# Attention over a 32,768-key cache on one core: the values of heads 8, 12 and 16 loaded by GpSimd's queue instead of SP's

## The chip, the cores and the metric

The kernel runs on one core of one Trainium2 chip. Time is device microseconds from the start to the end of the program. TensorE is called PE, VectorE DVE, ScalarE ACT, GpSimd POOL and SyncE SP. SP computes nothing here; it issues DMA transfers, which 16 DMA engines carry out.

## The reference

One decoding step for one token: a layer norm, attention with 32 heads over a cache, and a small dense block behind it. Only the first part matters here.

```python
def _A_ref(x, k_cache, v_cache, wq, wo):
    B, Sq, D = x.shape                     # 1, 1, 512
    H, Dh = 32, 128                        # k_cache, v_cache: (1, 32, 32768, 128)
    q = (x @ wq).reshape(B, Sq, H, Dh).transpose(0, 2, 1, 3)
    scores = jnp.einsum("bhqd,bhkd->bhqk", q, k_cache) * (Dh ** -0.5)
    p = _softmax(scores, axis=-1)
    o = jnp.einsum("bhqk,bhkd->bhqd", p, v_cache)
    return o.transpose(0, 2, 1, 3).reshape(B, Sq, H * Dh) @ wo

h = x + _A_ref(_layernorm(x), k_cache, v_cache, wq, wo)
return h + _B_ref(_layernorm(h), w1, b1, w2)   # 512 -> 1376 -> 512
```

All tensors are bf16. Each head reads 8.39 MB of keys and as much of values, each once: 537 MB over 32 heads.

## The kernel before

**Tiles.** SBUF holds a ring of six slots of 128 partitions x 16,384 values. The keys of one head fill two slots, and there are two such homes for keys, taken by even and odd heads. The values of one head fill two more slots, and there is one home for values (`V_HOME`). Partition p holds the rows 256 p to 256 p + 255 of the head, so a partition's share is one run of 64 KB in memory and in SBUF.

**Work of one head h.** `head(h)`: PE transposes the 256 key blocks (`k_group`, into tile `tps`), DVE copies each eight of them to SBUF (tile `ering`), and PE multiplies these by the query into the scores (`scores`, tile `sps`). DVE then takes the maximum. `rest`: while the exponentials of head h-1 are ready, PE runs the product with the values of head h-1 (`pv`, 256 matmuls into tile `ops`, "PV" below), with the small matmuls of the softmax of head h in between; then ACT makes the exponentials of head h (tile `pbuf`). So PE's order is: keys of head h, PV of head h-1, keys of head h+1, PV of head h, and so on.

**The order of the loads.** The list `order` in the builder gives it: the query weights (`WQ`), the keys of head 0, and then, for each h from 1, the keys of h and the values of h-1. In `program`, SP goes through this list. Before each load it waits until the buffer is free: keys of head h+2 wait for the transposes of head h (`freed_by`), values of head h wait for the end of PV of head h-1 (the event `pv{h-1}`, through `done_with`). `start` then issues the load, which raises the semaphore `ready[slot]` by 16 when it has landed. SP issues in list order: while it waits for one buffer, nothing behind it in the list is issued. PE waits on `ready[V_HOME]` before the first matmul of PV, against a count that `fills` gives for each load.

Some loads at the beginning and the end are cut in pieces (`pieces`); those of heads 8, 12 and 16 are whole.

**POOL** has two small steps at the start of the program (`iota`, `memset`) and one multiplication near its end (`hu`).

## Time and profile before

| | |
|---|---|
| time, median of 2 runs | 1275.15 us (1275.08 to 1275.23) |
| profiled execution, span from the first to the last instruction | 1273.1 us |
| mean granted PE clock | 0.766 |
| read from memory | 548.09 MB, 431 GB/s over the span |
| busy: PE, DVE, ACT, POOL | 1019.9, 718.2, 20.6, 0.9 us |

The profile gives for its execution the span alone; the median of the runs is 2.05 us above it. How to read the rows: an engine's name with a "q" (SPq) is its instruction queue, here the issuing of DMAs; "tile <- tile" names what an instruction writes and reads; L551 is the line of the kernel at which it was issued (L551 is `start`, so all of SP's loads). A row of a waits view says which engine waited, at which line, for whom, how long in total, how many times, and the longest. "Landing" is when the last byte of a transfer has arrived, counted from its issue. "issue" as a releaser is time in which the engine waited for nothing that the profile shows.

### The profile page before, as it was taken

The page shows a single profiled execution, that of the slowest core. Times are in us where ns is not written, and L with a number is a line of the kernel's source. Part 1 is how long each engine was busy: PE and PEld are TensorE (multiplying, and loading weights), DVE is VectorE, ACT ScalarE, POOL GpSimd, SP SyncE. Part 2 cuts the span into 40 slices and gives each one's busy share as a digit, 9 for nine tenths or more (in the row PEclk, how much of TensorE's full clock was granted, in tenths as well). Part 3 has the DMA queues.
Part 4 walks back from the last instruction along what each step waited for, and adds up shares of the span by engine and source line. Part 5 has one row for each costly group of instructions (what it writes and reads, how often), then busy time and mean ns, then how long its engine had stood idle before and what let it go on. Part 6 is the DMA issues. An engine that isn't in the chain of part 4 may idle for free.

```text
span 1273.1 us, 54451 instructions
## 1 busy us (share of the span) xinstructions
PE 1019.9 (80%) x25046; PEld 993.3 (78%) x25047; DVE 718.2 (56%) x1257; ACT 20.6 (2%) x71; POOL 0.9 (0%) x7
## 2 busy tenths in 40 slices
PE   4789877779777789777798777797777897777996
PEld 4789877779777779777788777797777887777994
DVE  3656664456654456644566544566545666444661
ACT  0000000000000000000000000000000000000000
POOL 0000000000000000000000000000000000000000
PEclk9778877678877778776788777788767887777885
DMA  9999999999999999999999999999999999999998
GB/s 406 442 417 438 432 439 432 432 434 430 432 441 428 437 434 428 432 439 432 434 434 430 430 439 434 430 434 434 428 434 441 428 437 432 430 432 439 427 427 360
DMA packets 12214, 548.22 MB, mean 431 GB/s; under 512 B 1348, under 2 KB 1454, under 8 KB 2862
## 3 DMA queue, kind: packets, MB, share of 16 engines
q1 hardware_dynamic: 12204, 548.09, 99.7%
q8 instruction: 8, 0.13, 0.0%
q10 hardware_dynamic: 2, 0.00, 0.0%
HBM read 548.09 MB, written 0.00 MB: 431 GB/s over the span
## 4 chain that ended last, share of the span: by engine, by line
DMA 54%; DVE 23%; PE 19%; issue 2%; SPq 2%; POOL 0%; POOLq 0%
DMA ring<-in_A_k_cache_dram 51%; DVE ering L696 23%; PE ops L717 9%; PE tps L690 7%; DMA ring<-in_A_v_cache_dram 2%; SPq L551 2%; PE sps L666 1%; DMA ring<-in_B_w_dram 1%; PE hlp L741 1%; PE hlp L736 1%; PE hlp L751 0%; PE tps L867 0%; DVE pmax L730 0%; DVE perm L872 0%; DVE gmax L738 0%
## 5 line engine op out<-in xcount | busy, mean ns | idle before, releaser
L690 PE MATMUL tps<-identb,ring 128*128 128x128 bf16 x8192 | 671.7, 233 | 208.8 <-DMA ring<-in_A_k_cache_dram 203.2
L696 DVE COPY ering<-tps 128x1024 bf16<-128x1024 bf16 x1024 | 669.7, 691 | 261.6 <-PE tps L690 261.1
L690 PEld LDWEIGHTS tps<-identb,ring 128*128 x8192 | 525.4, 105 | 211.6 <-issue 211.6
L666 PE MATMUL sps<-qcur,ering 128*128 128x1 bf16 x8192 | 343.7, 164 | 7.3 <-DVE ering L696 6.6
L666 PEld LDWEIGHTS sps<-qcur,ering 128*128 128x128 bf16 x8192 | 309.4, 97 | 10.1 <-DVE ering L696 9.4
L717 PEld LDWEIGHTS ops<-pbuf,ring 128*128 128x128 bf16 x8192 | 226.4, 103 | 23.3 <-issue 15.1
L717 PE MATMUL ops<-pbuf,ring 128*128 128x1 bf16 x8192 | 231.3, 165 | 10.6 <-DMA ring<-in_A_v_cache_dram 7.2
L725 DVE TENSOR_TENSOR oT<-ops,rtotc 128x1 f32 x31 | 5.0, 161 | 110.6 <-PE ops L717 110.6
L738 DVE TENSOR_REDUCE gmax<-hlp 1x1 f32<-1x128 f32 x32 | 8.9, 279 | 64.5 <-PE hlp L736 64.5
L743 DVE TENSOR_SCALAR nbias<-hlp 128x1 f32<-128x1 f32 x32 | 5.1, 158 | 63.5 <-PE hlp L741 63.5
L746 ACT ACTIVATE pbuf<-sps,nbias 128x256 bf16<-128x256 f32 x32 | 15.2, 474 | 1219.7 <-PE ops L717 1166.8
L730 DVE TENSOR_REDUCE pmax<-sps 128x1 f32<-128x256 f32 x32 | 13.6, 424 | 14.3 <-PE sps L666 14.3
L736 PE MATMUL hlp<-ident,pmax 128*1 128x128 f32 x64 | 17.1, 363 | 2.5 <-issue 2.5
L741 PE MATMUL hlp<-gmax,onesmat 1*128 1x1 f32 x64 | 18.5, 356 | 0.4 <-DVE gmax L738 0.4
L741 PEld LDWEIGHTS hlp<-gmax,onesmat 1*128 1x128 f32 x64 | 15.8, 304 | 1.3 <-DVE gmax L738 0.9
L751 PE MATMUL hlp<-esum,onesmat 128*128 128x1 f32 x64 | 12.1, 259 | 4.7 <-issue 0.6
L751 PEld LDWEIGHTS hlp<-esum,onesmat 128*128 128x128 f32 x64 | 9.8, 191 | 7.1 <-issue 7.1
L645 PE MATMUL hlp<-xnT,ring 128*128 128x1 bf16 x128 | 3.6, 165 | 9.2 <-DMA ring<-in_A_wq_dram 9.2
L645 PEld LDWEIGHTS hlp<-xnT,ring 128*128 128x128 bf16 x128 | 3.5, 104 | 9.3 <-issue 9.3
L725 DVE TENSOR_TENSOR oL<-ops,rtotc 128x1 bf16<-128x1 f32 x1 | 0.2, 161 | 12.4 <-PE ops L717 12.4
L649 DVE CAST qT<-hlp 128x32 bf16<-128x32 f32 x1 | 0.2, 192 | 11.5 <-PE hlp L645 11.5
L746 ACT ACTIVATION_READ_ACCUMULATOR pbuf<-sps,nbias 128x1 f32 x32 | 6.2, 193 | 0.0
(82 smaller groups left out, 45.5 us busy)
## 6 DMA issues: line engine op xcount, KB each, us to landing
ring<-in_A_k_cache_dram SPq DMA_DIRECT2D x3, 4096.0 KB, 40.0
ring<-in_A_v_cache_dram SPq DMA_DIRECT2D x3, 4096.0 KB, 16.0
ring<-in_A_k_cache_dram SPq DMA_DIRECT2D x3, 2048.0 KB, 30.9
ring<-in_A_k_cache_dram SPq DMA_DIRECT2D x1, 6144.0 KB, 45.2
ring<-in_A_wq_dram SPq DMA_DIRECT2D x1, 4096.0 KB, 12.3
ring<-in_A_wo_dram SPq DMA_DIRECT2D x1, 4096.0 KB, 35.1
ring<-in_A_v_cache_dram SPq DMA_DIRECT2D x1, 2048.0 KB, 16.1
ring<-in_B_w_dram SPq DMA_DIRECT2D x4, 344.0 KB, 20.5
```

Of the source, the lines that this page charges most:

```text
L551: S.dma(SP, lambda: sp.dma_start(dst, src).then_inc(s, 16))
L645: S.step(PE, lambda h=h, kc=kc: t_.matmul(Q_REG[:, h:h + 1], wq_v[:, kc, h * Dh:(h + 1) * Dh], xnT[:, 0, kc:kc + 1], start=(kc == 0), stop ...
L666: S.step(PE, lambda r=r: t_.matmul(S_ps[:, col0 + r:col0 + r + 1], ering[:, bg % NE, r, :], qcur[:, :], start=True, stop=True), name=(name ...
L690: S.step(PE, lambda r=r, at=at: t_.matmul(tb[:, r * 128:(r + 1) * 128], key_tile(S, at), identb[:, :], is_transpose=True, start=True, stop ...
L696: S.step(DVE, lambda: v.tensor_copy(ering[:, bg % NE, :, :].rearrange("p r d -> p (r d)"), tb[:, :]), name=f"ev{bg}", waits=[f"trb{bg}"], ...
L717: S.step(PE, lambda r=r: t_.matmul(o_ps[:, 0:1], vt[:, r, :], pbuf[:, r:r + 1], start=(r == 0), stop=(r == SCOLS - 1)), name=(names or Non ...
L730: S.step(DVE, lambda: v.tensor_reduce(pmax[:, :], S_ps[:, 0:SCOLS], AXX, ALU.max), name=f"pmax{h}", waits=[f"qkh{h}"], kind="pmax")
L736: S.step(PE, lambda: t_.matmul(A_REG, pmax[:, :], ident[:, :], start=True, stop=True), name=f"A{h}", waits=[f"pmax{h}", "ident", f"rcp{h - ...
L738: S.step(DVE, lambda: v.tensor_reduce(gmax[:, :], A_REG, AXX, ALU.max), name=f"gmax{h}", waits=[f"A{h}"], kind="gmax")
L741: S.step(PE, lambda: t_.matmul(B_REG, onesm[0:1, :], gmax[:, :], start=True, stop=True), name=f"B{h}", waits=[f"gmax{h}", "consts0"] + ([] ...
L746: S.step(ACT, lambda: a.activation(pbuf[:, :], S_ps[:, 0:SCOLS], ACTF.Exp, bias=nb[:, :], scale=SC, accum_out=esum[:, :]), name=f"exp{h}", ...
L751: S.step(PE, lambda: t_.matmul(C_REG, onesm[:, :], esum[:, :], start=True, stop=True), name=f"C{h}", waits=[f"exp{h}"], kind="C")
```

## The change

Three heads, 8, 12 and 16, are named in `BY_POOL`. When SP comes to their values in the list it skips them: it neither waits for PV of the head before nor issues the load. POOL, after its two steps at the start, goes through the three: it waits for PV of head h-1, issues the load of v(h) on its own DMA queue with a semaphore of its own, waits until that has landed, and then raises `ready[V_HOME]` by 16, which is what SP's load would have raised. For the last of the three, head 16, SP waits in its list, at the place of the skipped load, until all three of POOL's loads have landed; the next in the list are the keys of head 18.

```diff
+    BY_POOL = (8, 12, 16)
+    s_pool = sem("by_pool")
+
     events = {}
...
             else:
                 kind, h = what
+                if kind == "v" and h in BY_POOL:
+                    if h == BY_POOL[-1]:
+                        S.wait(SP, [(s_pool, 16 * len(BY_POOL))])
+                    continue
                 rows = keys_of(A_k_cache if kind == "k" else A_v_cache, h)
                 for r0, r1 in pieces(what):
...
         S.step(POOL, lambda: g.iota(identi[:, :], [[-1, 128]], base=0, channel_multiplier=1), name="iota")
         S.step(POOL, lambda: g.memset(b1r[:, :], 0.0), name="b1z")
+        for n, h in enumerate(BY_POOL):
+            S.dma(POOL, lambda h=h: g.dma_start(tiles_of(("v", h)), keys_of(A_v_cache, h)).then_inc(s_pool, 16), waits=[f"pv{h - 1}"])
+            S.wait(POOL, [(s_pool, 16 * n + 16)])
+            S.dma(POOL, lambda: g.sem_inc(ready[V_HOME], 16))
```

## The prediction

> **What bounds the kernel now.** First the page: how full the DMA engines are, and what the chain of waits is made of.

> ```profile
> span 1273.1 us, 54451 instructions
> ...
> PE 1019.9 (80%) x25046; PEld 993.3 (78%) x25047; DVE 718.2 (56%) x1257; ACT 20.6 (2%) x71; POOL 0.9 (0%) x7
> ...
> q1 hardware_dynamic: 12204, 548.09, 99.7%
> ...
> DMA 54%; DVE 23%; PE 19%; issue 2%; SPq 2%; POOL 0%; POOLq 0%
> ```

> One queue, SP's (q1), carries 548 MB and keeps the 16 DMA engines busy for 99.7% of the span. The chain shows DVE and PE too, because it runs through them to the moment at which a buffer comes free and SP may issue again. So the bound is the transfers, as long as the queue never runs dry. How full it is over two heads in the middle (DMA share, then GB/s, at the end of the row):

> ```profile
> core 0: us, PE busy (x) PEld busy (x) DVE busy (x) ACT busy (x) POOL busy (x), PEclk, DMA share, GB/s
> ...
> 588.00:665.90 77.90, 62.84 (x1550) 61.55 (x1548) 44.39 (x76) 1.13 (x4) 0.00 (x0) 0.76 1.00 434
> ```

> Share 1.00 at 434 GB/s: a head's keys, or its values (256 x 128 x 128 bf16, 8.39 MB), take 8.39 / 434 = **19.3 us**, a head 38.7. Now SP's issues (timeline of its queue), and how long each takes to land:

> ```profile
> 16.71 0.33 SPq L551 DMA_DIRECT2D ring<-in_A_v_cache_dram  x1
> ...
> 355.90 0.33 SPq L551 DMA_DIRECT2D ring<-in_A_v_cache_dram  x1
> 356.33 0.38 SPq L551 DMA_DIRECT2D ring<-in_A_k_cache_dram  x1
> ...
> 511.33 0.33 SPq L551 DMA_DIRECT2D ring<-in_A_v_cache_dram  x1
> ...
> 665.87 0.33 SPq L551 DMA_DIRECT2D ring<-in_A_v_cache_dram  x1
> 666.30 0.38 SPq L551 DMA_DIRECT2D ring<-in_A_k_cache_dram  x1
> ```

> ```profile
> issues: line engine op xcount, KB each, median us to landing
> ...
> ring<-in_A_wq_dram SPq DMA_DIRECT2D x1, 4096.0 KB, 12.3
> ...
> ring<-in_A_v_cache_dram SPq DMA_DIRECT2D x30, 26.1
> ring<-in_A_k_cache_dram SPq DMA_DIRECT2D x29, 44.9
> ```

> Counting V issues from head 0 at 16.71 us, the last three here are heads 8, 12 and 16. Call t = 0 the end of PV of head h-1, when SP issues v(h) and, 0.43 us later, k(h+2). v(h) lands at 26.1, so 26.1 - 19.3 = 6.8 us of k(h+1) were still ahead of it; k(h+2) lands at 0.43 + 44.9 = 45.3. The order in the queue is k(h+1), v(h), k(h+2). Last, what PE does between a key landing and the next issue (chain of waits, one head):

> ```profile
> 588.50 45.34 DMA ring<-in_A_k_cache_dram
> 633.84 0.40 issue
> 634.24 3.59 PE tps L690 x32
> ...
> 657.51 0.38 PE hlp L751 x2
> 657.89 1.63 PE ops L717 x64
> ...
> 662.34 3.52 PE ops L717 x128
> 665.86 0.02 issue
> 665.87 0.33 SPq L551
> ```

> From landing, 0.4 us to PE's start, then 634.24 to about 657.65 for transposes and scores (23.4), then PV to 665.86 (8.2): 32.0 together. A key landing at 6.8 gives the next end of PV at 6.8 + 32.0 = 38.8, one head's period. At that moment the queue still holds 45.3 - 38.8 = 6.5 us of work. This reserve is what the change can spend for nothing.

> **The change, part by part.** Removed: three V issues of 0.33 us on SP, which is waiting almost always; worth 0.

> Moved, heads 8 and 12: the V load goes to POOL's own queue, behind the same end of PV(h-1). SP no longer waits there, so it runs on to k(h+2), which waits only for the transposes of head h, done before the 657.51 of the chain, over 8 us before t = 0. There k(h+1) is still being moved, so the earlier issue lies behind it in a full queue and is worth 0 by itself. What it alters is the order: at t = 0 SP's queue holds 6.8 us of k(h+1) and 19.3 of k(h+2), and v(h) starts beside them instead of between them. Total work is the same and engines are full, so both queues are empty at 45.3 as before; but v(h), which PE needs first, now shares.

> When does it start? No POOL DMA is in this trace. Two rows bound it, the first loads of the program into idle engines:

> ```profile
> 0.74 0.51 ACTq L601 DMA_DIRECT2D xr<-in_A_x_dram  x1
> 0.75 0.39 SPq L882 DMA_DIRECT2D ring<-in_A_wq_dram  x1
> ```

> ```profile
> GB/s 0 0 0 0 0 0 0 0 0 0 0 0 0 0 0 0 0 0 0 0 0 0 0 0 0 0 0 0 0 0 0 0 20 0 0 1966 655 1966 655 1966
> DMA packets 13, 0.36 MB, mean 181 GB/s; under 512 B 1, under 2 KB 2, under 8 KB 2
> ```

> That is 0 to 2 us in slices of 0.05: the 1 KB on ACT's queue, issued at 0.74, moves at 1.60, the weights of SP, issued at 0.75, at 1.75: about 0.9 to 1.0 us. Issue to landing of those 4096 KB (4.19 MB, 9.7 us at 434) took 12.3, 2.6 too much. POOL's start lies between 0.9 and 2.6; I take 1.5, nearer the first since only the start counts. It is not below 0.9 unless POOL beats both queues, which nothing shows. [...]

> How do two queues share? The trace has one contest, instruction fetches (q8) against SP's full queue: PE's waits from 30 to 100 us, and the queues from 36 to 52.

> ```profile
> PE tps L690 <- issue: 4.8, 3, 3.2
> ...
> PE ops L717 <- issue: 3.4, 1, 3.4
> ```

> ```profile
> q1 hardware_dynamic: 234, 7.14, 103.8%
> q8 instruction: 2, 0.03, 0.8%
> ```

> A fetch gets through in at most 3.4 us while SP's loads of 9.7 to 19.3 us are under way: neither at the end of the load nor after all that is queued. In the middle stretch a data packet is 64 KB:

> ```profile
> DMA packets 582, 33.95 MB, mean 435 GB/s; under 512 B 64, under 2 KB 64, under 8 KB 64
> ```

> (33.95 MB over 582 - 64 packets.) At 434/16 GB/s one takes 2.4 us, within a fetch's delay. So I take turns by packet, with POOL's packets as large as SP's since it copies the same 64 KB rows: **half each**. Then from 1.5 on:

> - k(h+1): 5.3 us left at half rate, landed at 1.5 + 10.6 = 12.1; PE through with its scores at 12.1 + 0.4 + 23.4 = 35.9;
> - v(h): 1.5 + 2 x 19.3 = 40.1, PE takes it up at 40.5 (POOL's passing on of the landing I price at 0; SP resumes 0.02 us after what it waits for, in the chain above); PV ends at 48.7;
> - the queues ran dry at 45.3, and SP issues v(h+1) and k(h+3) only at 48.7: 3.4 us idle, plus the restart, 2.6 by the first load (1.0 if only the first byte counts): **6.0 us**, twice, **12.0**.

> Nothing of it comes back: the following head finds its key landed, v(h+1) lands at 48.7 + 2.6 + 19.3 = 70.6, before the scores end at 72.1, PV ends at 80.3, and k(h+3) lands near 90, so the queue has its reserve again and the path is DMA once more. Each loss of DMA time adds to the end.

> Moved and added, head 16: SP waits for v(16) to land; behind that wait stand k(18), v(17) and every later load. k(17) and v(16) are 26.1 us of work, so v(16) lands at 26.1 in whatever shares. k(18) is issued then, into empty queues: a restart, **2.7 us** with 0.1 for the wake-up (1.1 to 2.7). k(17) is late at 12.1, PV(16) ends at 35.9 + 8.2 = 44.1; k(18) lands at 26.2 + 2.6 + 19.3 = 48.1, so v(17) is issued before the queue is dry: no second gap. The cover is 4.0 us; past it each us costs one.

> Added on POOL: three issues, waits and signals. The only POOL work behind them is one product near the end (waits by length):

> ```profile
> POOL hsb L859 <- DVE hsb L858: 1267.0, 1, 1267.0
> ```

> It comes over 500 us later; 0.

> Sum: 12.0 + 2.7 = **14.7 us**: 1273.1 of span becomes 1287.8; the median lies 2.05 above that span, so 1275.15 + 14.7 = **1289.9**. With the ends of start and restart it is 8.7 (5.4 - 1.6 = 3.8, twice, and 1.1) to 16.9 (7.1 twice and 2.7).

> **The rivals.** *POOL gets less than its half.* With smaller packets than SP's, or a late start (descriptors written slowly, anything over 6.7 us), v(h) comes last of all. From a share of 19.3 / (45.3 - 1.5) = 0.44 down it lands when both queues are dry, at 45.3; PV ends at 45.3 + 0.4 + 8.2 = 53.9, so 8.6 + 2.6 = 11.2, twice, and 2.7: 25.1, **1300.2**. A start so late also opens a gap at head 16. For it: 0.50 is close to 0.44, and POOL's packets have no row. Against: a fetch of 16 KB packets is not starved.

> *POOL is served first*, the side slower than 2%. v(h) lands at 20.8, but all of k(h+1) that was left waits until 26.1; scores end at 49.9, PV at 58.1: 12.8 + 2.6 = 15.4. Head 16 is no better: k(18) goes out at 20.9 and lands by 45.3, PV(16) ends at 58.1. Three times 15.4 is 46.2, **1321.4**. It decides once POOL's share passes 0.55 (scores and v(h) then meet near 37) and grows to this at 1. For it: the fetch, also a second queue, was quick. Against: it is one packet, which tells nothing of a long run of them.

> *The engines take turns by whole loads.* Each finishes its part of k(h+1), then takes v(h), then k(h+2): the order of before, and nothing lost at heads 8 and 12; head 16's 2.7 remain: **1277.9**. For it: nothing but the arithmetic. Against: the fetches of at most 3.4 us, where half a load would be 9.7. [...]

> *Faster* needs two queues to move more than 434 GB/s, and the DMA share is already 1.00.

> **How the numbers follow.** Half shares 0.50 (its own range 1279 to 1295, shares of 0.47 to 0.55 taken in: at 0.47 v(h) lands at 42.6, 2.5 later, twice); less than half or late 0.24; POOL first 0.10; whole loads 0.13; anything else 0.03. The range 1277 to 1303 leaves out POOL first, the later starts and a little else, about 0.2. Two per cent, about what a measurement can tell from no change, is 25.5 us, 1300.65: slower takes POOL first and over half of the late case, whose 1300.2 sits at the line: 0.24. Faster 0.01. Within 2%: 0.75.

> **What would show it.** In the profile after: two PE waits of some 4 to 5 us for values of heads 8 and 12, a gap of DMA share of about 5 us after each, key packets of about 4.8 us instead of 2.4 beside a POOL queue of 25 MB, and one gap of 2 to 3 us before k(18). v(8) landing near 26 would make it whole loads, near 45 the late case, near 21 with PE waiting for keys instead POOL first. A POOL transfer that starts more than 3 us after its release, or a total below 434 GB/s with both queues full, would break the sum.

## The result, and the profile after

The changed kernel takes 1295.33 us (1294.88 to 1295.77), a ratio of 1.0158 with a 95% interval of 1.0139 to 1.0177: 20.2 us slower, within two per cent and clear of noise, where 14.7 was forecast. The span of its profiled execution is 1293.1 us, 20.0 above that of before. The page after, in the lines that answer to those of before:

```profile
span 1293.1 us, 54454 instructions
...
q1 hardware_dynamic: 11772, 522.92, 93.8%
q0 software_dynamic: 432, 25.17, 4.5%
...
DMA 54%; DVE 23%; PE 20%; issue 2%; SPq 0%; POOL 0%; ACT 0%; POOLq 0%
```

A second queue, q0, now carries POOL's three loads (25.17 MB). Together the two queues keep the DMA engines busy for 98.3% of the span, against 99.7% before: the missing 1.4 points are 18 of the 20 us. Where they are, by who waited for whom:

```profile
PE tps L701 <- DMA ring<-in_A_k_cache_dram: 201.4, 28, 9.6
...
PE ops L728 <- POOLq L617: 20.4, 2, 10.3
```

PE waits twice, 20.4 us in all, for POOL to report values (L617 is the line of its signal). At head 16 it does not. The chain of waits around head 8, from the release of POOL's load to the next end of PV:

```profile
356.29 0.30 issue
356.58 42.89 DMA ring<-in_A_v_cache_dram
399.48 0.03 issue
399.50 0.03 POOLq L617
...
404.26 3.50 PE ops L728 x128
407.76 0.77 issue
```

v(8) lands 43.2 us after its release at 356.29 (40.1 was forecast, 26.1 before), POOL passes this on in 0.1, and PV ends at 51.5 (forecast 48.7). Meanwhile the queues ran dry. The DMA view from 396 to 412 us, in slices of 0.4 us, a packet counted where it starts:

```profile
DMA  9779079700000000000000000000000999800009
```

The last packets start at about 399 us and take 2.4 (the time of a 64 KB packet: the 15 in the row of q0 below take 113.5% of 16 engines' 2 us); the next start at about 408.4, after PV. Head 12 is alike: from 519.84 to 571.09 is 51.25. Head 16, where SP holds the next keys back (L554 is SP's load):

```profile
683.28 0.28 issue
683.56 25.50 DMA ring<-in_A_v_cache_dram
709.06 0.02 issue
709.08 21.94 DMA ring<-in_A_k_cache_dram
731.02 0.40 issue
```

v(16) lands 25.8 us after its release (forecast 26.1), and k(18) takes 21.94 into empty queues, 2.6 more than 19.3. At head 8, too, the load that SP issues into the empty queues, v(9), lands 22.0 us after its issue, 2.7 more than 19.3.

The sum with these numbers: head 8 costs 51.5 - 45.3 + 2.6 = 8.8, head 12 costs 51.25 - 45.3 + 2.6 = 8.6, head 16 costs 731.02 - 683.28 - 45.3 = 2.4. Together 19.8 of the 20.0 in the spans.

When do the packets of POOL's queue begin? The queues of the DMA view, first from 356.3 to 360.7 us, then from 360.7 to 362.7:

```profile
q1 hardware_dynamic: 27, 1.77, 92.9%
```

```profile
q0 software_dynamic: 15, 0.98, 113.5%
```

Up to 360.7 all is SP's. In the next 2 us every packet that begins is POOL's: 4.4 to 6.3 us after the release, where the prediction had 1.5. (At head 12 they begin at 525.4 to 526.1, 5.6 to 6.3 after the release.) Since then the queues share. From 364 to 384 us:

```profile
q0 software_dynamic: 67, 4.39, 50.7%
q1 hardware_dynamic: 74, 4.19, 48.5%
```

Half each, as was forecast. So what was wrong in the forecast is the start. At all three heads the first POOL packets followed on the last packets of k(h+1), and three readings fit that: POOL is slow to set its load going; a queue gets its first turn only when the load in front has ended; or engines that are busy take up a new queue later than idle ones.

### The profile page after: what moved, and what is told of

The parts are those of the page before. It is cut to its first block, busy times and chain, and to the rows that moved or that the text cites. A ratio compares the mean times of both kernels' runs of the same rounds, so it can differ in the third digit from the quotient of the medians.

```text
span 1293.1 us, 54454 instructions
## 1 busy us (share of the span) xinstructions
PE 1018.5 (79%) x25046; PEld 991.4 (77%) x25047; DVE 717.9 (56%) x1257; ACT 20.6 (2%) x71; POOL 2.7 (0%) x10
## 3 DMA queue, kind: packets, MB, share of 16 engines
q0 software_dynamic: 432, 25.17, 4.5%
HBM read 548.09 MB, written 0.00 MB: 424 GB/s over the span
## 4 chain that ended last, share of the span: by engine, by line
DMA 54%; DVE 23%; PE 20%; issue 2%; SPq 0%; POOL 0%; ACT 0%; POOLq 0%
DMA ring<-in_A_k_cache_dram 42%; DVE ering L707 23%; DMA ring<-in_A_v_cache_dram 12%; PE ops L728 10%; PE tps L701 7%; PE sps L677 1%; PE hlp L752 1%; PE hlp L747 1%; PE hlp L762 0%; SPq L554 0%; PE tps L878 0%; PE sps L858 0%; PE hlp L843 0%; DVE pmax L741 0%; DVE perm L883 0%
## 5 line engine op out<-in xcount | busy, mean ns | idle before, releaser
L728 PE MATMUL ops<-pbuf,ring 128*128 128x1 bf16 x8192 | 231.5, 165 | 31.8 <-POOLq L617 20.4
L741 DVE TENSOR_REDUCE pmax<-sps 128x1 f32<-128x256 f32 x32 | 13.6, 424 | 14.3 <-PE sps L677 14.3
L736 DVE TENSOR_TENSOR oL<-ops,rtotc 128x1 bf16<-128x1 f32 x1 | 0.2, 161 | 13.6 <-PE ops L728 13.6
L660 DVE CAST qT<-hlp 128x32 bf16<-128x32 f32 x1 | 0.2, 190 | 11.4 <-PE hlp L656 11.4
L747 PEld LDWEIGHTS hlp<-ident,pmax 128*1 128x1 f32 x64 | 2.7, 81 | 4.8 <-issue 4.3
## 6 DMA issues: line engine op xcount, KB each, us to landing
ring<-in_A_k_cache_dram SPq DMA_DIRECT2D x3, 4096.0 KB, 40.2
ring<-in_A_v_cache_dram SPq DMA_DIRECT2D x3, 4096.0 KB, 15.8
ring<-in_A_wq_dram SPq DMA_DIRECT2D x1, 4096.0 KB, 12.3
ring<-in_A_wo_dram SPq DMA_DIRECT2D x1, 4096.0 KB, 35.9
ring<-in_B_w_dram SPq DMA_DIRECT2D x4, 344.0 KB, 20.6
```

The lines of the kernel that those rows point to most:

```text
L728: S.step(PE, lambda r=r: t_.matmul(o_ps[:, 0:1], vt[:, r, :], pbuf[:, r:r + 1], start=(r == 0), stop=(r == SCOLS - 1)), name=(names or Non ...
L736: S.step(DVE, lambda: v.tensor_tensor(out_column(), o_ps[:, 0:1], rtotc[:, :], ALU.mult), name=f"oev{h}", waits=[f"pv{h}", f"rcp{h}"], kin ...
L741: S.step(DVE, lambda: v.tensor_reduce(pmax[:, :], S_ps[:, 0:SCOLS], AXX, ALU.max), name=f"pmax{h}", waits=[f"qkh{h}"], kind="pmax")
L747: S.step(PE, lambda: t_.matmul(A_REG, pmax[:, :], ident[:, :], start=True, stop=True), name=f"A{h}", waits=[f"pmax{h}", "ident", f"rcp{h - ...
```

## The experiments

Each edit is shown against the changed kernel, unless it says otherwise.

**No head held back, and all of them.** Do the two kinds of loss have the prices of the sum?

```diff
                 if kind == "v" and h in BY_POOL:
-                    if h == BY_POOL[-1]:
-                        S.wait(SP, [(s_pool, 16 * len(BY_POOL))])
                     continue
```

> SP no longer waits for v(16); head 16 goes as heads 8 and 12. Theory A: POOL's load starts 4.4 to 5.8 us after its release and then takes every second packet turn, so each load not held back costs 8.7 us (6.2 of empty queues and 2.5 of restart). Three of them: 1275.15 + 26.1 = 1301.3, and PE's wait for POOL at line 617's counterpart is there three times, about 10 us each. Rival B: head 16's wait costs as much as the other two (the 20.2 us are three equal parts of 6.7): 1295.3, unchanged.

1303.29 us (1300.69 to 1303.79), ratio 1.0215 (1.0198 to 1.0232). PE's waits for POOL:

```profile
PE ops L726 <- POOLq L615: 29.5, 3, 10.5
```

Three waits of about 10 us now: head 16, not held, costs as the others do. 28.1 us over three is 9.4 each, a little above the 8.7 of the sum.

```diff
                 if kind == "v" and h in BY_POOL:
-                    if h == BY_POOL[-1]:
-                        S.wait(SP, [(s_pool, 16 * len(BY_POOL))])
+                    S.wait(SP, [(s_pool, 16 * (BY_POOL.index(h) + 1))])
                     continue
```

> SP waits for the landing at all three heads. Theory A: POOL's late start does not matter as long as k(h+1) is still moving, the only loss is a restart of 2.6 to 2.7 us each: 1275.15 + 8.1 = 1283.2; PE never waits for values. Rival B (three equal parts): 1295.3.

1283.26 us (1282.86 to 1285.12), ratio 1.0069 (1.0052 to 1.0085): 8.1 us, 2.7 a head, as expected. The waits view has no row of PE waiting for POOL. In the chain at head 8 the landing and the restart stand one after the other, as at head 16 above:

```profile
356.60 25.83 DMA ring<-in_A_v_cache_dram
...
382.45 21.87 DMA ring<-in_A_k_cache_dram
```

So head 16's wait is the cheaper of the two forms by about 6 us; three equal parts are excluded.

**The next keys held back until v(h) has moved alone for a while.** If only the sharing of the engines costs, and not POOL, then nothing should be lost when k(h+2) comes late, but before v(h) is through.

```diff
-                    if h == BY_POOL[-1]:
-                        S.wait(SP, [(s_pool, 16 * len(BY_POOL))])
+                    S.wait(SP, [free_name(("k", h + 1, 0))])
                     continue
```

> At all three heads SP holds k(h+2) until the first half of the transposes of head h+1 is done, about 20 us after POOL's release, when v(h) is still moving alone. Theory A: v(h) moves 15 us alone and shares only its last 4, lands near 28 us, before the scores end at 33, and the queues are never empty: no loss, 1275.2 (1274.5 to 1277), with all three loads still on POOL. If the writing of descriptors by POOL or its queue as such were the cost (rival C), two thirds of the loss or more would stay: 1288 or more.

1277.62 us (1274.98 to 1278.94), ratio 1.0017 (1.0007 to 1.0027): 17.7 of the 20.2 us are gone with all three loads still on POOL. The landing of POOL's loads, from the DMA issues:

```profile
ring<-in_A_v_cache_dram POOLq DMA_DIRECT2D x3, 28.2
```

28.2 us, against 42.7 in the changed kernel, and again no row of PE waiting for POOL. The remaining 2.5 us were expected to be nil or at most 1.9. The page shows no emptied queues behind them: q1 is at 95.1% and q0 at 4.6%, 99.7% of the span as before. From 350 to 700 us the full engines move 432 GB/s where they moved 434 before, which would be 1.6 us of it, an estimate as far as three digits tell; why they are slower isn't settled.

**ACT's queue in place of POOL's for heads 8 and 12.** Is the late start POOL's own?

```diff
-    BY_POOL = (8, 12, 16)
+    BY_ACT = (8, 12)
+    BY_POOL = (16,)
...
+                if kind == "v" and h in BY_ACT:
+                    continue
                 if kind == "v" and h in BY_POOL:
...
         def soft_exp(h):
+            if h in BY_ACT:
+                S.dma(ACT, lambda: a.dma_start(tiles_of(("v", h)), keys_of(A_v_cache, h)).then_inc(ready[V_HOME], 16), waits=[f"pv{h - 1}"])
```

> v(8) and v(12) are issued on ACT's queue in place of POOL's; head 16 stays as in the changed kernel (2.7 us). Theory A (the start 4.4 us or more after the release is POOL's path): ACT's load starts about 1 us after the release, takes its turns beside the end of k(h+1), lands at 38 to 40.5 instead of 43; each costs 4.5 to 6.4 us, together 1287 to 1291. Rival D (the load waits until SP's load in front has ended, whatever the queue): the start stays at 4.7 to 5.8 us, each costs 8.7: 1295.3.

1294.05 us (1290.83 to 1296.04), ratio 1.0154 (1.0137 to 1.0171): above the range that the theory gave, and the interval (1292.6 to 1296.9 us) takes in the rival's figure, so the time alone doesn't decide. Its four runs lie 5.2 us apart, and the profiled execution is the fastest of them, 1290.83, so its rows speak for the start and not for the median. Its DMA view at head 8, released at 356.00, from 356 to 359.4 and from 359.4 to 361.4 us (q10 is ACT's queue):

```profile
q1 hardware_dynamic: 20, 1.31, 89.0%
```

```profile
q10 hardware_dynamic: 16, 1.05, 121.1%
```

ACT's packets begin 3.5 to 5.2 us after the release, not 1 us. That takes most of the late start away from POOL: on idle engines ACT's small load began 0.9 us after its issue (in the prediction's rows). It also speaks against the rival: the keys in front are not through when ACT's packets begin, they are put off by them, and PE's longest wait for keys is 12.5 us here, against 9.6 in the changed kernel. v(8) and v(12) land 41.9 and 40.6 us after their issue, about 1 and 2 us earlier than POOL's.

**POOL into idle engines.** The kernel before, with the first load on POOL and SP's others held back until it has landed:

```diff
-    nc.sync.dma_start(ring[:, slot_of(WQ), :], A_wq.rearrange("(p k) n -> p (k n)", k=KC)).then_inc(ready[slot_of(WQ)], 16)
...
                 S.wait(SP, ["b1z"])
+                S.wait(SP, [ready_wait(WQ)])
...
+        S.dma(POOL, lambda: g.dma_start(ring[:, slot_of(WQ), :], A_wq.rearrange("(p k) n -> p (k n)", k=KC)).then_inc(s_pool, 16))
...
+        S.wait(POOL, [(s_pool, 16)])
+        S.dma(POOL, lambda: g.sem_inc(ready[V_HOME], 16))
```

> The kernel before, with its first load (the query weights, 4096 KB) issued by POOL and SP's other loads held back until it has landed, so POOL's load starts into idle engines. Theory T (POOL's path is about 2 us from release to first packet, the rest of the 4.7 to 5.8 is waiting for turns): first packet 1.7 to 2.2 us after the issue, landing at 13.0 to 13.6 where SP's took 12.3. Rival A (POOL's path alone takes 4.4 us or more): landing at 15.7 or later. The time is about 13 to 16 us above the kernel before, since nothing else moves meanwhile.

```profile
1.24 0.71 POOL L607 DMA_DIRECT2D ring<-in_A_wq_dram  x1 [0.79 <-POOLq L911]
```

```profile
GB/s 0 0 0 0 0 0 0 0 20 0 0 0 0 0 0 0 0 0 0 0 0 0 0 0 0 0 0 0 0 2621 1311 1966 1311 0 655 655 0 0 0 655
```

The second row is 1.2 to 3.2 us in slices of 0.05: POOL's packets begin at 2.65 by this view, 1.4 us after the issue. The load lands at 12.6 us where SP's took 12.3. So a load issued by GpSimd is 0.3 us slower from issue to landing, and rival A falls. (The time, 1279.10, is 3.9 us above the kernel before, not 13 to 16. That expectation was a slip: the query weights are moved ahead of the rest in both kernels. POOL's issue is 0.5 us later than SP's was, the landing takes 0.3 more, and a restart of 2.6 would make it 3.4, an estimate.)

**Half rows.** Do engines share by packet or by byte? Each of POOL's loads in two, of half rows, so that a packet is 32 KB:

```diff
-            S.dma(POOL, lambda h=h: g.dma_start(tiles_of(("v", h)), keys_of(A_v_cache, h)).then_inc(s_pool, 16), waits=[f"pv{h - 1}"])
-            S.wait(POOL, [(s_pool, 16 * n + 16)])
+            for r0, r1 in ((0, TPS), (TPS, SCOLS)):
+                S.dma(POOL, lambda h=h, r0=r0, r1=r1: g.dma_start(tiles_of(("v", h))[:, r0:r1, :], keys_of(A_v_cache, h)[:, r0:r1, :]).then_inc(s_pool, 16),
+                      waits=[f"pv{h - 1}"])
+            S.wait(POOL, [(s_pool, 32 * n + 32)])
```

(SP's wait at head 16 counts 32 for each head accordingly.)

> As the changed kernel, but each of POOL's loads is two loads of half rows, so that its packets are 32 KB and SP's stay at 64 KB. Theory T (engines take turns packet by packet, whatever their size; a new queue's first packet waits for the one in transfer and one more): POOL gets a third of the bytes, v(h) lands last of all, at 45 to 46 us after its release, and heads 8 and 12 cost about 11.4 each: 1275.15 + 22.8 + 2.7 = 1300.6 (1299 to 1303). Rival B (queues share bytes evenly): the landing stays at 43 and the time at 1295.3.

1299.60 us (1299.45 to 1300.19), ratio 1.0193 (1.0176 to 1.0210). The queues from 364 to 384 us:

```profile
q1 hardware_dynamic: 87, 5.70, 65.9%
q0 software_dynamic: 85, 2.79, 32.3%
```

87 packets against 85, and 5.70 MB against 2.79: turns were taken packet by packet. v(8) lands 45.3 us after its release at 356.53 (the chain has it from 357.54, 44.29 us), last of all, as the prediction's first rival would have it.

**Values of head 0 by POOL**, beside SP's packets of 16 and 32 KB:

```diff
-    BY_POOL = (8, 12, 16)
+    BY_POOL = (0,)
...
-                if kind == "v" and h in BY_POOL:
-                    if h == BY_POOL[-1]:
-                        S.wait(SP, [(s_pool, 16 * len(BY_POOL))])
-                    continue
...
-                    start(tiles_of(what)[:, r0:r1, :], rows[:, r0:r1, :], s)
+                    if what != ("v", 0):
+                        start(tiles_of(what)[:, r0:r1, :], rows[:, r0:r1, :], s)
...
-            S.dma(POOL, ..., waits=[f"pv{h - 1}"])
+            S.dma(POOL, ..., waits=freed_by(("v", 0)))
```

> Only the values of head 0 go by POOL, released at 16.7 us, while SP's queue holds about 33 us of keys in packets of 32 KB. Theory T: the wait for two of SP's packets shrinks with them, first packet about 3.2 to 4.5 us after the release, and with 64 KB against 32 KB POOL gets two thirds: its 8 packets per engine are through after 8 x 3.6 = 29 us, landing at 32 to 35 us after the release. Rival B (even bytes): landing at 42 or later. Rival A (fixed start of 4.4 us or more): first packet at 4.4 to 5.8. The keys of heads 0 and 1 come later, which costs time of its own: 1280 to 1300.

1286.22 us. The queues from 24 to 46 us, and POOL's landing:

```profile
q0 software_dynamic: 111, 7.27, 76.4%
q1 hardware_dynamic: 107, 2.56, 27.0%
```

```profile
ring<-in_A_v_cache_dram POOLq DMA_DIRECT2D x1, 33.2
```

Again one packet for one (16 of SP's 107 are under 512 B: more on these at the last run below), now in POOL's favour, and 33.2 us to landing as theory T had it. Its other half fails: with SP's packets at half the size the first POOL packets still begin at 20.7 to 22.2 us, 4.1 to 5.6 after the release at 16.6, hardly earlier than beside 64 KB. The delay here was not a count of packets in front.

**Keys of head 10 by POOL**, released in the middle of k(9), and all values by SP:

```diff
-    BY_POOL = (8, 12, 16)
+    BY_POOL = (10,)
...
-                if kind == "v" and h in BY_POOL:
-                    if h == BY_POOL[-1]:
-                        S.wait(SP, [(s_pool, 16 * len(BY_POOL))])
+                if kind == "k" and h in BY_POOL:
                     continue
...
-            S.dma(POOL, lambda h=h: g.dma_start(tiles_of(("v", h)), keys_of(A_v_cache, h)).then_inc(s_pool, 16), waits=[f"pv{h - 1}"])
+            S.dma(POOL, lambda h=h: g.dma_start(tiles_of(("k", h)), keys_of(A_k_cache, h)).then_inc(s_pool, 16), waits=freed_by(("k", h)))
             S.wait(POOL, [(s_pool, 16 * n + 16)])
-            S.dma(POOL, lambda: g.sem_inc(ready[V_HOME], 16))
+            S.dma(POOL, lambda h=h: g.sem_inc(ready[slot_of(("k", h))], 16))
```

> Only the keys of head 10 go by POOL, released when the transposes of head 8 are done, some 9 us before the end of PV(7) and with about 16 us of k(9) left on SP's queue; all values go by SP. Theory T: POOL's first packet comes 4.4 to 6.8 us after the release, in the middle of k(9), whose landing is put off; PE waits 17 to 18 us for k(9) where it waited 7, v(8) lands last at 45 after PV(7), one loss of 11.2: 1286.3 (1283 to 1288). Rival D (a queue gets its first turn when the load in front has ended): the first packet 14 to 16 us after the release and PE's wait for k(9) at 7 to 10.

1287.66 us. POOL's issue, the two queues from 352 to 366 us, and PE's wait for keys:

```profile
346.88 0.72 POOL L613 DMA_DIRECT2D ring<-in_A_k_cache_dram  x1 [345.56 <-PE tps L699]
```

```profile
q1 hardware_dynamic: 48, 3.15, 51.9%
q0 software_dynamic: 47, 3.08, 50.8%
```

```profile
PE tps L699 <- DMA ring<-in_A_k_cache_dram: 214.7, 30, 19.6
```

POOL's packets begin at 350.9 to 353.0 us, 4.0 to 6.1 after the issue, while k(9) is being moved, and from then on the two queues take turns. k(9) is put off: PE waits 19.6 us for it (17 to 18 expected; 7.8 was the longest before). POOL's queue did not wait for the load in front to end: rival D falls. The last PE wait, for v(8), ends 45.9 us after its issue, and 12.5 us are lost where 11.2 were expected.

**Four loads of 32 partitions each**, to see whether a semaphore write takes a turn:

```diff
-            S.dma(POOL, lambda h=h: g.dma_start(tiles_of(("v", h)), keys_of(A_v_cache, h)).then_inc(s_pool, 16), waits=[f"pv{h - 1}"])
-            S.wait(POOL, [(s_pool, 16 * n + 16)])
+            for p in range(0, 128, 32):
+                S.dma(POOL, lambda h=h, p=p: g.dma_start(tiles_of(("v", h))[p:p + 32], keys_of(A_v_cache, h)[p:p + 32]).then_inc(s_pool, 16),
+                      waits=[f"pv{h - 1}"])
+            S.wait(POOL, [(s_pool, 64 * n + 64)])
```

(SP's wait at head 16 counts 64 for each head.)

> As the changed kernel, but each of POOL's loads is four loads of 32 partitions: the same 64 KB packets, 8 per engine, and four semaphore writes per engine instead of one. Theory T with a semaphore write taking a whole turn: three turns more, v(h) lands when everything else has, at about 45.4, heads 8 and 12 cost about 11.2 each: 1300.3 (1298 to 1302). Rival S (a semaphore write takes no turn of its own): landing at 43, 1295.3. If POOL's late start came from writing many descriptors, its first packet would now come earlier by a good part of the 4.7 to 5.8 us.

1397.99 us (1383.20 to 1398.75), ratio 1.0927 (1.0865 to 1.0989). Neither theory: another effect hides the question in the time. The other point of the expectation can be read: POOL's first packet begins at 360.25, 3.9 us after the issue at 356.34, against 4.2 in the changed kernel, with a quarter of the rows in the first load. If the late start grew with the rows of the load, a good part of it should have gone. At head 16 POOL's load moves alone, from 775 to 805 us:

```profile
core 0: us, PE busy (x) PEld busy (x) DVE busy (x) ACT busy (x) POOL busy (x), PEclk, DMA share, GB/s
775.00:805.00 30.00, 23.71 (x514) 23.46 (x514) 21.61 (x35) 0.00 (x0) 0.00 (x0) 0.84 0.94 194
```

Share 0.94, and only 194 GB/s: these loads of 32 neighbouring partitions moved at less than half the 434 GB/s of SP's loads of 128.

Whether a semaphore write takes a turn can be read from the changed kernel instead. Its queues from 363 to 394 us:

```profile
DMA packets 222, 13.50 MB, mean 435 GB/s; under 512 B 16, under 2 KB 16, under 8 KB 16
...
q0 software_dynamic: 110, 7.21, 53.7%
q1 hardware_dynamic: 112, 6.29, 46.9%
```

The 16 packets under 512 B are SP's: 6.29 MB are the other 96 at 64 KB. I read the 16 as the semaphore writes of k(9), whose landing raises its semaphore by 16. The turns are even, 110 to 112, only if these count, and POOL moves 14 rows more than SP. At head 12 the order shows it. POOL's first 16 rows begin by 526.1; from 526.5 to 529.5 begin POOL's second 16 and 16 packets of SP without bytes; from 529.5 to 531.5 come 16 rows of SP alone. So, if the 16 are the semaphore writes, each took a turn and waited for POOL's row as a packet of 64 KB does. That put off the report of k(13): its last rows began before 525.2, and PE waited for it until 529.2, 9.4 us, where it waited 6.7 before.

## Why the prediction was right or wrong

- **The bound and the measure of it**: right. Emptied queues are nearly all of the cost: 8.8, 8.6 and 2.4 us by the chain make 19.8 of 20.0, and holding k(h+2) back so that the queues never empty returns all but 2.5.
- **Half shares, turns by packet**: right, and shown from both sides (87 to 85 packets with bytes at 2 to 1, 111 to 107 with bytes at 1 to 2.8). The late case was a real one next door: with packets of 32 KB it came as priced, 1299.6 against 1300.2. The turns by whole loads are excluded. In these runs a turn was one row of 64 KB or 32 KB, for POOL's queue too.
- **The restart, 2.6**: right; 21.94 - 19.3 in the changed kernel.
- **Head 16, 2.7**: right; 2.4 by the chain, and 8.1 for three in a run of their own.
- **The start of POOL's load, 1.5 within 0.9 to 2.6**: this term failed. It began at 4.4 to 6.3, so v(8) landed 3.1 us later than forecast and each of heads 8 and 12 cost 8.7 in place of 6.0: 2 x 2.7 = 5.4, the whole of what lies between 1289.9 and 1295.3. The rows it was taken from were of loads into idle engines, and there they hold for POOL as well: 1.4 us from issue to first packet. Into busy engines ACT's load begins at 3.5 after its issue at the earliest (0.9 for its 1 KB load into idle ones), POOL's at 3.8 to 4.2: both queues are about 2.6 us later there. The last of the 16 engines begins up to 2.1 us after the first (keys of head 10), less than the 2.4 us that a 64 KB packet takes. That GpSimd issues the load is a small part, 0.5 us, the difference of the two queues on idle engines.
- **The landing of k(h+1), 12.1**: too late. PE's waits for these keys, 9.6 and 9.4 us, end about 9 to 10 us after the release, since POOL's rows began only behind the last rows of k(h+1); what is above the 6.8 is, by the order at head 12, the turn that the 16 packets read as its semaphore writes waited for. The scores of head 8 were through 33 us after the release, not 35.9. It cost nothing, as v(h) came later still, but with the late v(h) it made PE's waits 10.3 and 10.1 us, where 4 to 5 were announced.
- **The range** held the time, and that is in part luck. The prediction's own ends of start and restart gave a loss of at most 16.9, and half shares a time of at most 1295; 20.2 and 1295.3 lie above both. A start of more than 3 us after the release was to break the sum, and it did. The range held because it reached past the late rival's 1300.2; a start between 2.6 and 6.7, as measured, stood in no sum of the prediction. Its two per cent line, 1300.65, was not crossed. The rival of POOL being served first has no support in any run.

What the 2.6 us are isn't settled, so the cause of the late start stays open. They hardly shrink with SP's packets at half the size (a first packet 4.1 us after the release, against 4.4), so they are not one packet in front; beyond that no run here shows where they go.

## What to carry to other kernels

A second DMA queue beside a full one added no bandwidth here (432 GB/s from 361 to 399.5 us with both queues full, 434 with one) and took the order out of SP's hands: the engines gave each queue one packet in turn (87 to 85 in the run of half rows), so the transfer that was needed first got its share by the ratio of packet sizes (5.70 MB to 2.79). Keep what must arrive in order on one queue, or hold the later load back until the urgent one has had its time alone, but not until it has landed, which cost a restart of 2.7 us a head here. And price the start of a load from a row where the engines are as busy as they will be (POOL's first packet came 4.0 us after the issue into busy ones, 1.4 into idle ones).
